# The skip weights of an S4D convolution, added by VectorE in SBUF in place of an identity matmul in PSUM

## The chip, the cores and the metric

The kernel runs on one core of one Trainium2 chip. Its five engines work side by side, each through its own queue of instructions in order: TensorE (PE in the profile; its weight loads are PEld), VectorE (DVE), ScalarE (ACT), GpSimd (POOL) and SyncE (SP, which here issues DMAs alone). The metric is the device time of one execution in microseconds (us).

## The reference

A layer norm of `x` (2048 tokens of 448 channels), and on its output `xn` two branches that are summed with `x`:

```python
xn = layernorm(x)
# branch A: a long convolution whose kernel comes from 256 complex modes per channel
A = -exp(log_A_real) + 1j * A_imag;  C = (C_real + 1j * C_imag) * dt
K = 2.0 * einsum("dn,dnl->dl", C, exp(A * dt * pos)).real      # 448 x 2048
y = irfft(rfft(xn, 2L) * rfft(K, 2L))[:L] + xn * D_skip
# branch B: a gated unit, 448 -> 1792 -> 448
h = (sigmoid(xn @ w_gate) * (xn @ w_up)) @ w_down
out = x + y + h
```

`xn * D_skip` is the same as adding `D_skip` to tap 0 of the convolution's kernel `K`, and that is how the kernel does it.

## The kernel before

Two generators in Python are traced in turns: `glu()` (branch B) and `conv()` (branch A). `conv` prepares the modes (`prep`), makes the kernels `K` (`kgen`), and then works in the frequency domain (`spectra`). Weights that are handed to the turns (`WK`, `WS` and others) decide how far one generator is traced before the other goes on. All instructions then get their place in their engine's queue from a planner that simulates the execution with its own costs: of the instructions that are ready it issues the one with the highest priority, which is the order of tracing, changed in places by `high_priority` blocks (`hp(HP)`) and by `issue_after` (behind a given instruction of the same engine). So the queue of an engine need not have the order of the code. Where an instruction needs what another engine has not finished, it waits at the head of its queue, and what is queued behind it waits too.

`kgen` makes the 448 kernels in 56 chunks of 8 channels, and 4 chunks make a bank of 32 channels, so there are 14 banks. Of a tap with index l = 64 a + b the two parts are made apart. For one chunk:

- GpSimd builds powers of the modes' magnitudes, `me` and `mf`, by doubling (`magnitudes`, L495 and L507), for two chunks at a time; ScalarE fills part of `me` by squares (L520).
- PE turns phases into angles (`ahead`, L529, tile `tr`), ScalarE takes sines (L537 to L540, tile `S`).
- DVE multiplies magnitudes by sines: `Et` in two instructions (L591, L592), `Ft` in one (L593). `Et` has two buffers, `Ft` has one.
- PE sums over the modes: 64 small matmuls into the PSUM tile `ko` (L607), 8 channels beside each other. `ko` holds a bank: 4 groups of 32 partitions (`a`) by 8 slots of 64 columns (`b`).

After the fourth chunk of a bank, the matmul at L617 adds the skip weights to the bank in PSUM: the stationary operand is a 128x128 identity, the moving one `dm[:, bank]`, 128x8, in which the rows 0, 32, 64 and 96 hold the `D_skip` of the bank's channels and all others are zero. It adds to column 0 of each slot, which with row 0 of each group is tap 0. ScalarE copies the bank to the SBUF tile `ks` (L620), of which there is one buffer. `first_stage` (L555) is the first step of the Fourier transform: 128 matmuls that read `ks`, traced two chunks later, or at once, with raised priority, for the last bank. ScalarE copies its results to `sk` (L561) and stores them in DRAM (L562). `spectra` loads them from there (`skl`) for the second step (L892).

Meanwhile `glu` has PE do the products of the gated unit, with its operands split into a high and a low part: L699 (tile `gu`) and L810 (tile `po`). On DVE it has the gate (L710), low parts of activations and weights (L717 `hl`, L754 `wl`) and the sums of the output (L815); on ScalarE the tanh (L707) and high parts (L715 `hh`, L750 `wh`); on GpSimd some weights' parts (L761, L762, L780).

Of the kernel before, what the change touches and what calls it, by code (L numbers as in the profile page):

```python
# [15 lines left out]
ALU = mybir.AluOpType  # L16
# [34 lines left out]
NCK = D // DC  # L51
# [77 lines left out]
def s4d_glu_kernel(ctx, tc, io):  # L129
    nc = tc.nc  # L130
    hp = tc.high_priority
    v = nc.vector
# [17 lines left out]
    ident = const.tile([128, 128], F32, name="ident")  # L150
# [10 lines left out]
    dm = const.tile([128, D // 32, 8], F32, name="dm")  # L161
# [272 lines left out]
    def powers(pms, g, fts, behind=None):  # L434

        w = W1s[0][:, NCH * g : NCH * g + NCH].rearrange("p g h e -> p (g h e)")
        pm = pms[g % 2]
        with tc.issue_after(behind.ins) if behind else nullcontext():
            nc.scalar.activation(pm[:, 0], w, AF.Identity, bias=one)
        for js, o in (((1, 2, 3), None), ((4, 5, 7), slice(1, 6)), ((8, 9), None), ((10, 11), slice(7, 12))):  # L440
            with tc.issue_after(fts[0].ins) if behind else nullcontext():
                for j in js:
                    v.scalar_tensor_tensor(pm[:, j], w, 2.0, w, ALU.add, ALU.mult)
                    w = pm[:, j]
                if o:
                    nc.scalar.activation(pm[:, o], pm[:, o], AF.Identity, bias=one)
            yield

    def kgen(pk):
# [11 lines left out]
        tl = {n: pk.tile(sh, dt_, name=n) for n, sh, dt_ in late}  # L461
# [22 lines left out]
        def magnitudes(b):  # L484

            c = 2 * b % NCH
            o = slice(2 * DC * c, 2 * DC * c + 4 * DC)
            pm = pms[2 * b // NCH % 2]
            par = lambda i: pm[:, i, o]
            me = mes[b % 2]  # L490
            mf = tl[f"mf{b % 2}"]
            gg = GGs[0][:, 2 * b : 2 * b + 2].rearrange("p c h e -> p (c h e)")

            with tc.issue_after(mls[0].ins) if mls else nullcontext():
                nc.gpsimd.tensor_tensor(  # L495
                    mf[:, :, 0:2],
                    gg.unsqueeze(2).to_broadcast([128, 4 * DC, 2]),
                    pm[:, 6:8, o].rearrange("p i m -> p m i"),
                    ALU.mult,
                )  # L500
            for m, base, nst in ((me, 0, 6), (mf, 7, 5)):
                for i in range(1 if m is mf else 0, nst):
                    w = 1 << i

                    a, n = (1, 2) if m is me and i > 3 else (0, 1)
                    with tc.issue_after(mls[0].ins) if mls else nullcontext():
                        ins = nc.gpsimd.tensor_tensor(  # L507
                            m[:, :, w + a : 2 * w : n],
                            m[:, :, a:w:n],
                            par(base + i).unsqueeze(2).to_broadcast([128, 4 * DC, w // n]),  # L510
                            ALU.mult,
                        )
            mls[:] = [ins]
            return me, mf

        def squares(me):

            with tc.issue_after(sins[0].ins) if sins else nullcontext():
                for w in (16, 32):
                    nc.scalar.activation(me[:, :, w : 2 * w : 2], me[:, :, w // 2 : w], AF.Square)  # L520

        def ahead(cn):


            S = tl[f"S{cn % 2}"]
            ps = psc[-1].tile([128, 2, 512], F32, name="tr", bufs=1)
            ph = pht[cn // 2 % 2]
            for h in range(2):
                nc.tensor.matmul(  # L529
                    ps[:, h], ph[:, cn % 2, 128 * h : 128 * h + 128], sel, start=True, stop=True  # L530
                )
            if cn % 2 == 1 and cn + 3 < NCK:
                phase_load(cn // 2 + 2)
            rows = lambda t: t.rearrange("p c (h e) s -> p h c (e s)", h=2)
            pv = ps.rearrange("p h (c x) -> p h c x", c=2)
            cs = S[:, 1:4:2]
            nc.scalar.activation(rows(cs), pv, AF.Abs)  # L537
            nc.scalar.activation(rows(S[:, 0:5:4]), pv, AF.Sin, scale=TWO_PI)
            nc.scalar.activation(rows(S[:, 2:3]), pv[:, :, 0:1], AF.Sin, scale=-TWO_PI)
            sins[:] = [nc.scalar.activation(cs, cs, AF.Sin, scale=-TWO_PI, bias=hpi)]  # L540
            return S

        def first_stage(bank):

            ks, sk = tl["ks"], tl["sk"].rearrange("p k (s r j) -> p r k s j", r=2, j=2)

            pss = [
                psc[-1].tile([128, 8, 2, 32], F32, name="kp", bufs=1),
                psg.tile([128, 8, 2, 32], F32, name="kq", tag="gu", bufs=4),
            ]  # L550
            for s_ in range(8):
                for cc in range(2):
                    for r in range(2):
                        rows = slice(64 * r, 64 * r + 64)
                        nc.tensor.matmul(  # L555
                            pss[r][64 * cc : 64 * cc + 64, s_].rearrange("p j k -> p (j k)"),
                            ks[rows, s_], wk[rows, cc], start=True, stop=True,
                            skip_group_check=True,
                        )
            for r in range(2):  # L560
                nc.scalar.copy(sk[:, r], pss[r].rearrange("p s j k -> p k s j"))  # L561
            nc.scalar.dma_start(sk_d[:, bank], tl["sk"])  # L562
# [11 lines left out]
        for g in range(NCK // NCH):  # L574
            for c in range(NCH):
                cn = g * NCH + c
                S = nxt
                me, mf = (m[:, 2 * DC * (c % 2) : 2 * DC * (c % 2) + 2 * DC] for m in mags)
                if c == 2 and NCH * (g + 1) < NCK:
                    more = powers(pms, g + 1, fts, sins[0])  # L580
                if 2 <= c < 6 and NCH * (g + 1) < NCK:
                    next(more)
                if cn + 1 < NCK:
                    nxt = ahead(cn + 1)
                    if c % 2 == 1:
                        squares(coming[0])
                yield WK / 3
                Et = tl[f"Et{cn % 2}"]
                Ft = tl["Ft"]
                two = lambda ap: ap.unsqueeze(1).to_broadcast([128, 2, 2 * DC, 32])  # L590
                v.tensor_tensor(Et[:, :, :, 32:64], two(me[:, :, 32:64]), S[:, 1::-1], ALU.mult)  # L591
                v.tensor_tensor(Et[:, :, :, 0:32], two(me[:, :, 0:32]), S[:, 1:3, :, ::-1], ALU.mult)  # L592
                fts[:] = [v.tensor_tensor(Ft, two(mf), S[:, 3:5], ALU.mult)]  # L593
                if cn + 2 < NCK and c % 2 == 0:
                    coming = magnitudes(cn // 2 + 1)
                if c % 2 == 1:
                    mags = coming
                yield WK / 3
                if cn % 4 == 0:
                    ko = psc[-1].tile([128, 8, 64], F32, name="ko", bufs=1)  # L600
                with tc.issue_after(glu_mm[0].ins):
                    for q in range(2):
                        sl = 2 * (cn % 4) + q
                        for k in range(4):
                            h, cc = k // 2, k % 2
                            for j in range(4):
                                nc.tensor.matmul(  # L607
                                    ko[32 * j : 32 * j + 32, sl],
                                    Ft[:, cc, DC * h + 4 * q + j],
                                    Et[:, cc, DC * h + 4 * q + j],  # L610
                                    start=(k == 0),
                                    stop=(k == 3),
                                    skip_group_check=True,
                                )
                if cn % 4 == 3:
                    ks = tl["ks"]
                    nc.tensor.matmul(  # L617
                        ko[:, :, 0], ident, dm[:, cn // 4], start=False, stop=True, skip_group_check=True
                    )
                    nc.scalar.copy(ks, ko)  # L620
                yield WK / 3
                if cn % 4 == 2 and cn > 3 or cn + 1 == NCK:

                    with hp(HP) if cn + 1 == NCK else tc.issue_after(glu_mm[0].ins):
                        first_stage((cn - 3) // 4 if cn + 1 < NCK else cn // 4)
# [520 lines left out]
```

## Time and profile before

| | |
|---|---|
| median of 3 runs | 735.8 us (734.0 to 740.97) |
| the profiled execution | 732.29 us |
| its span, first to last instruction | 730.4 us |
| PE busy | 679.1 us, 93% |
| DVE busy | 560.4 us, 77% |
| ACT busy | 421.1 us, 58% |
| POOL busy | 379.7 us, 52% |

The span is from the first to the last instruction of the profiled execution; 1.9 us lie around it. A row of the timeline has an instruction's start and length in us, its engine and line, what it writes and reads, and in brackets the idle time of its engine before it and what ended that. Lengths of matmuls overlap, since they are pipelined. A row of waits has who waited for whom, the total in us, how often, and the longest.

### The profile page before, as it was taken

What the parts mean: (1) busy time and instruction counts of PE and PEld (TensorE: products, weight loads), DVE (VectorE), ACT (ScalarE), POOL (GpSimd) and SP (SyncE); (2) the same over time, 40 slices, a digit from 0 to 9 for tenths busy, and PEclk for the clock granted to TensorE, in tenths of its full rate; (3) what the DMA queues carried; (4) which work ended last, traced back from release to release, by engine and by line L of the source; (5) the groups of instructions that cost most, each with busy time, mean ns of one, the idle gap of its engine ahead of it and who ended that gap; (6) DMA issues with size and microseconds to landing.
All of it is one profiled execution on the core that took longest, in us unless ns stands there. A gap on an engine that the chain in (4) does not pass through costs nothing.

```text
span 730.4 us, 19084 instructions
## 1 busy us (share of the span) xinstructions
PE 679.1 (93%) x7780; PEld 534.4 (73%) x7780; DVE 560.4 (77%) x776; ACT 421.1 (58%) x650; POOL 379.7 (52%) x423
## 2 busy tenths in 40 slices
PE   2998799997999999888999999999999999999994
PEld 1765688785887787555878887888877787776783
DVE  5799996798899999889579969977855555564553
ACT  3646364677688787888567778776742222323310
POOL 2120036798788987974655875876844002351001
PEclk9998999997999999999999999999999999999998
DMA  9946338326313562635863242232269999999746
GB/s 209 227 107 201 79 104 273 128 95 197 125 51 110 184 201 68 189 114 178 224 172 123 76 144 84 83 110 68 78 164 271 248 245 243 251 242 249 182 135 162
DMA packets 93288, 116.76 MB, mean 160 GB/s; under 512 B 12177, under 2 KB 81169, under 8 KB 92945
## 3 DMA queue, kind: packets, MB, share of 16 engines
q1 hardware_dynamic: 83888, 95.08, 47.9%
q10 hardware_dynamic: 6736, 14.57, 6.5%
q0 software_dynamic: 2576, 5.90, 3.5%
q8 instruction: 61, 1.00, 0.6%
q14 instruction: 27, 0.21, 0.1%
HBM read 70.75 MB, written 44.76 MB: 158 GB/s over the span
## 4 chain that ended last, share of the span: by engine, by line
PE 60%; DVE 10%; POOL 8%; DMA 8%; ACT 7%; issue 4%; SPq 2%; ACTq 1%; POOLq 0%; DVEq 0%
PE gu L699 23%; PE po L810 15%; PE sp L892 7%; PE ko L607 5%; PE pv L919 4%; PE tr L529 3%; POOL me L507 3%; POOL mf L507 2%; DMA wraw<-in_B_w_up_dram 1%; DVE wl L754 1%; POOL dl L780 1%; PE kp L555 1%; DMA acc<-in_A_u_dram 1%; DMA v_d<-vt 1%; DVE Et L591 1%
## 5 line engine op out<-in xcount | busy, mean ns | idle before, releaser
L507 POOL TENSOR_TENSOR me<-me,pm 128x32 f32<-128x32 f32 (+1 forms) x168 | 141.4, 841 | 89.6 <-DVE Et L592 77.6
L507 POOL TENSOR_TENSOR mf<-mf,pm 128x64 f32<-128x64 f32 (+1 forms) x112 | 127.1, 1135 | 4.7
L699 PE MATMUL gu<-xh,wh 128*128 128x512 f32 x336 | 101.8, 410 | 1.4 <-ACT xh L218 1.4
L699 PE MATMUL gu<-xh,wl 128*128 128x512 f32 x336 | 96.0, 393 | 0.0
L699 PE MATMUL gu<-xl,wh 128*128 128x512 f32 x336 | 95.8, 390 | 0.0
L591 DVE TENSOR_TENSOR Et<-me,S 128x1024 f32<-128x1024 f32 x56 | 82.6, 1475 | 10.1 <-ACT S L540 7.2
L810 PE MATMUL po<-dh,hh 128*128 128x448 f32 x224 | 86.0, 384 | 3.4 <-DVE acc L815 2.5
L810 PE MATMUL po<-dl,hh 128*128 128x448 f32 x224 | 84.3, 376 | 1.1 <-POOL dl L780 1.1
L592 DVE TENSOR_TENSOR Et<-me,S 128x1024 f32<-128x1024 f32 x56 | 77.0, 1375 | 10.1 <-ACT me L520 9.9
L593 DVE TENSOR_TENSOR Ft<-mf,S 128x1024 f32<-128x1024 f32 x56 | 78.3, 1398 | 7.0 <-POOL mf L507 3.1
L810 PE MATMUL po<-dh,hl 128*128 128x448 f32 x224 | 83.0, 373 | 0.0
L537 ACT ACTIVATE S<-tr 128x1024 f32<-128x1024 f32 x56 | 57.8, 1032 | 41.5 <-PE tr L529 39.5
L715 ACT CAST hh<-hf 128x512 fp32r<-128x512 f32 x56 | 34.9, 623 | 76.8 <-DVE hf L710 60.8
L699 PEld LDWEIGHTS gu<-xh,wh 128*128 128x128 f32 x336 | 62.4, 193 | 19.8 <-issue 3.4
L699 PEld LDWEIGHTS gu<-xh,wl 128*128 128x128 f32 x336 | 63.5, 189 | 15.1 <-DVE pl L306 0.7
L607 PEld LDWEIGHTS ko<-Et,Ft 128*32 128x32 f32 x3584 | 54.4, 111 | 26.7 <-issue 13.0
L699 PEld LDWEIGHTS gu<-xl,wh 128*128 128x128 f32 x336 | 63.0, 188 | 14.0 <-issue 0.7
L607 PE MATMUL ko<-Et,Ft 128*32 128x64 f32 x3584 | 64.5, 222 | 8.1 <-DVE Ft L593 6.3
L540 ACT ACTIVATE S<-S,hpi 128x1024 f32<-128x1024 f32 x56 | 65.5, 1170 | 2.9 <-DMA acc<-in_A_u_dram 2.9
L815 DVE SCALAR_TENSOR_TENSOR acc<-po,acc 128x448 f32<-128x448 f32 x80 | 48.5, 617 | 22.6 <-PE po L810 22.5
L717 DVE TENSOR_TENSOR hl<-hf,hh 128x512 fp32r<-128x512 f32 x56 | 49.6, 886 | 19.6 <-ACT hh L715 19.6
L710 DVE SCALAR_TENSOR_TENSOR hf<-th,gu 128x512 f32<-128x512 f32 x56 | 38.1, 681 | 31.1 <-PE gu L699 25.9
(196 smaller groups left out, 1284.2 us busy)
## 6 DMA issues: line engine op xcount, KB each, us to landing
sk_d<-sk ACTq DMA_DIRECT2D x14, 512.0 KB
sx<-x_d SPq DMA_DIRECT2D x32, 224.0 KB
skl<-sk_d SPq DMA_DIRECT2D x16, 448.0 KB
vp<-v_d SPq DMA_DIRECT2D x16, 448.0 KB
v_d<-vt SPq DMA_DIRECT2D x62, 112.0 KB
wt_d<-wh SPq DMA_DIRECT2D x9, 512.0 KB
wt_d<-wl SPq DMA_DIRECT2D x9, 512.0 KB
wl<-wt_d SPq DMA_DIRECT2D x9, 512.0 KB
```

The costliest lines, as they stand in the source:

```text
L507: ins = nc.gpsimd.tensor_tensor(m[:, :, w + a : 2 * w : n], m[:, :, a:w:n], par(base + i).unsqueeze(2).to_broadcast([128, 4 * DC, w // n]) ...
L537: nc.scalar.activation(rows(cs), pv, AF.Abs)
L540: sins[:] = [nc.scalar.activation(cs, cs, AF.Sin, scale=-TWO_PI, bias=hpi)]
L591: v.tensor_tensor(Et[:, :, :, 32:64], two(me[:, :, 32:64]), S[:, 1::-1], ALU.mult)
L592: v.tensor_tensor(Et[:, :, :, 0:32], two(me[:, :, 0:32]), S[:, 1:3, :, ::-1], ALU.mult)
L593: fts[:] = [v.tensor_tensor(Ft, two(mf), S[:, 3:5], ALU.mult)]
L607: nc.tensor.matmul(ko[32 * j : 32 * j + 32, sl], Ft[:, cc, DC * h + 4 * q + j], Et[:, cc, DC * h + 4 * q + j], start=(k == 0), stop=(k == ...
L699: glu_mm[:] = [nc.tensor.matmul(ps, a_, b_, start=(n == 0), stop=(n == len(mm) - 1))]
L717: v.tensor_tensor(hl, hf, hh, ALU.subtract)
L810: glu_mm[:] = [nc.tensor.matmul(po, a_[:, bs], w_, start=(n == 0), stop=(n == 3 * fc - 1))]
L815: v.scalar_tensor_tensor(acc[:, b], po, 0.5, acc[:, b], ALU.mult, ALU.add)
L892: mm = nc.tensor.matmul(to, tb[:kk, t, 64 * c : 64 * c + 64], rhs, start=True, stop=True, skip_group_check=True,)
```

## The change

The identity matmul goes. In its place DVE adds `dm[:, bank]` to column 0 of each slot of `ks`, in SBUF, after ScalarE's copy and before `first_stage` reads it. For all banks but the last, the add is traced in the next bank's first chunk, ahead of its `Et`; for the last bank it is traced after the copy, ahead of `first_stage`. It has no `issue_after` and no raised priority.

```diff
+        def skip(bank):
+            v.tensor_tensor(tl["ks"][:, :, 0], tl["ks"][:, :, 0], dm[:, bank], ALU.add)
+
...
                 yield WK / 3
+                if cn % 4 == 0 and cn:
+                    skip(cn // 4 - 1)
                 Et = tl[f"Et{cn % 2}"]
...
                 if cn % 4 == 3:
                     ks = tl["ks"]
-                    nc.tensor.matmul(
-                        ko[:, :, 0], ident, dm[:, cn // 4], start=False, stop=True, skip_group_check=True
-                    )
                     nc.scalar.copy(ks, ko)
                 yield WK / 3
+                if cn + 1 == NCK:
+                    skip(cn // 4)
                 if cn % 4 == 2 and cn > 3 or cn + 1 == NCK:
```

## The prediction

> **What bounds the kernel now.** I read the page from the top: busy shares, slices, then the chain that ended last.
>
> ```profile
> span 730.4 us, 19084 instructions
> PE 679.1 (93%) x7780; PEld 534.4 (73%) x7780; DVE 560.4 (77%) x776; ACT 421.1 (58%) x650; POOL 379.7 (52%) x423
> ...
> PE   2998799997999999888999999999999999999994
> ...
> DVE  5799996798899999889579969977855555564553
> ...
> PE 60%; DVE 10%; POOL 8%; DMA 8%; ACT 7%; issue 4%; SPq 2%; ACTq 1%; POOLq 0%; DVEq 0%
> ```
>
> TensorE (PE) is busy 93% of the span and carries 60% of the chain; VectorE (DVE) is nearly full in the first half and half empty in the last quarter. So I cut the span by stages. The kernel generation that the change touches runs from about 143 to 545 us; the columns are busy time of PE, its weight loads, DVE, ACT and POOL, then the granted clock, DMA share and GB/s.
>
> ```profile
> 143.00:300.00 157.00, 147.56 (x2237) 119.13 (x2236) 147.67 (x149) 121.30 (x177) 131.60 (x127) 0.97 0.41 131
> 300.00:345.00 45.00, 40.30 (x601) 26.28 (x595) 38.32 (x47) 38.20 (x64) 33.67 (x40) 0.96 0.50 147
> 345.00:545.00 200.00, 196.44 (x2991) 161.99 (x2991) 161.18 (x168) 140.42 (x202) 136.94 (x154) 0.99 0.40 120
> 545.00:650.00 105.00, 105.00 (x746) 80.34 (x745) 56.22 (x111) 30.50 (x58) 24.77 (x31) 1.00 1.03 250
> ```
>
> From 345 us PE is 98% busy and DVE 81%: PE time removed there is span removed. From 143 to 300 us both stand at 94%: there a microsecond taken from PE can be lost to DVE. Why DVE matters there is in the view of waits:
>
> ```profile
> POOL me L507 <- DVE Et L592: 77.6, 22, 8.9
> ```
>
> GpSimd, which makes the magnitudes for the next chunks, waits 77.6 us in all for DVE's products to free its buffer. Anything that delays an `Et` product on DVE goes round this loop.
>
> **What the change removes.** In each of 14 banks one matmul with the identity goes, which runs as two instructions.
>
> ```profile
> L617 PEld LDWEIGHTS ko<-dm,ident x28: 186/188/189, 167.1 to 541.5; 128*128 128x128 f32 x28
> L617 PE MATMUL ko<-dm,ident x28: 256/266/277, 167.1 to 541.6; 128*128 128x8 f32 x28
> ```
>
> The durations overlap, so I price it by starts, at one bank with it and one chunk without (PE's timeline, start and length):
>
> ```profile
> 194.07 1.10 PE L607 MATMUL ko<-Et,Ft 128*32 128x64 f32 x64
> 195.10 0.73 PE L529 MATMUL tr<-sel,ph 128*128 128x512 f32 x2
> ...
> 200.41 1.10 PE L607 MATMUL ko<-Et,Ft 128*32 128x64 f32 x64
> 201.44 0.39 PE L617 MATMUL ko<-dm,ident 128*128 128x8 f32 x2
> 201.69 0.48 PE L529 MATMUL tr<-sel,ph 128*128 128x512 f32 x1
> ```
>
> Without it the next work starts 195.10 - 194.07 = 1.03 us after the chunk's sums began, with it 201.69 - 200.41 = 1.28: 0.25 us for a bank, 14 x 0.25 = 3.5 us of PE time. How much lies on the path? The first and the last such piece in the chain, the first with what follows it:
>
> ```profile
> 201.51 0.32 PE ko L617 x2
> 201.83 0.57 PE tr L529 x2
> ...
> 513.92 0.32 PE ko L617 x2
> ```
>
> Banks 1, 4 and 6 to 12, counted from 0, have such a piece: nine, from the one at 201.51 to the one at 513.92. I take 9 x 0.25 = **-2.2 us**; bounds 0 and -3.5. The evacuation to `ks` (L620) can also start 0.3 us sooner, which I cost at nothing: the first stage that reads `ks` runs later anyway, apart from banks 0 and 13.
>
> **What the change adds: 14 small adds on DVE.** The trace has no such add on `ks`, but `x_scales` has ops of the same 128x8 size. In DVE's timeline, two that depend on each other, then a small one between strangers:
>
> ```profile
> 40.90 0.17 DVE L256 TENSOR_TENSOR z<-ys 128x8 f32<-128x8 f32 x1
> 41.10 0.17 DVE L257 SCALAR_TENSOR_TENSOR z<-z,ve 128x8 f32<-128x8 f32 x1
> ...
> 43.74 0.16 DVE L260 SCALAR_TENSOR_TENSOR zs<-mv,ys 128x8 f32<-128x8 f32 x1
> 43.82 1.22 DVE L754 TENSOR_TENSOR wl<-wraw,wh 128x1024 fp32r<-128x1024 f32 x1
> ```
>
> A small op holds DVE for 0.08 us when its neighbour doesn't need it and for 0.20 us when it does. The add's neighbours on DVE don't read `ks`, but it waits for ACT itself, so I take its length, 0.17. From 345 us on DVE has slack to hide it (81% busy); before 300 us it has not. Five banks (0 to 4) lie there: 5 x 0.17 = **+0.9 us**; bounds 5 x 0.08 = 0.4 and 14 x 0.20 = 2.8.
>
> The Trainium skill, "VectorE: DVE Perf Modes", section "The DRAIN you can't avoid", speaks against the change: the next op does not start until the pipe has emptied, so the count of ops is what to keep down. By that rule each add would cost its whole dependent step, 2.8 us in all; the 0.08 us step above doesn't bear it out between strangers, and the sum keeps its 0.9.
>
> **The wait that comes with it.** DVE takes its queue in order, so an add whose `ks` isn't there holds the products behind it. What matters is where the planner puts it: the code traces it ahead of the `Et` products of the next bank's first chunk, the planner issues what is ready. In bank 1 (ACT, then DVE, then PE):
>
> ```profile
> 201.87 0.59 ACT L620 COPY ks<-ko 128x512 f32<-128x512 f32 x1 [1.46 <-PE ko L617]
> ...
> 200.05 1.22 DVE L592 TENSOR_TENSOR Et<-me,S 128x1024 f32<-128x1024 f32 x1
> 201.18 1.44 DVE L591 TENSOR_TENSOR Et<-me,S 128x1024 f32<-128x1024 f32 x1
> 202.54 1.66 DVE L593 TENSOR_TENSOR Ft<-mf,S 128x1024 f32<-128x1024 f32 x1
> ...
> 204.96 0.27 PE L555 MATMUL kp<-wk,ks 64*64 64x64 f32 x1
> ```
>
> Both products of chunk 8 were issued before `ks` was done at 202.46. Issued by readiness, the add falls between L591 and L593 at 202.5: no wait on DVE, and 2.3 us before the first stage of this bank reads `ks`. So I cost the wait at nothing in the first 13 banks. If that cover went, the bank would lose what stands under the second rival.
>
> The last bank is different. ACT, DVE, GpSimd, PE, and for comparison the same DVE op one tile later:
>
> ```profile
> 541.28 0.62 ACT L715 CAST hh<-hf 128x512 fp32r<-128x512 f32 x1 [2.67 <-DVE hf L710]
> 541.85 0.59 ACT L620 COPY ks<-ko 128x512 f32<-128x512 f32 x1
> ...
> 541.93 2.65 DVE L717 TENSOR_TENSOR hl<-hf,hh 128x512 fp32r<-128x512 f32 x1 [0.69 <-ACT hh L715]
> 550.34 0.69 DVE L717 TENSOR_TENSOR hl<-hf,hh 128x512 fp32r<-128x512 f32 x1 [0.69 <-ACT hh L715]
> ...
> 541.66 2.36 POOL L762 TENSOR_TENSOR wl<-wraw,wh 128x1024 fp32r<-128x1024 f32 x1
> ...
> 542.49 0.27 PE L555 MATMUL kp<-wk,ks 64*64 64x64 f32 x1 [0.68 <-ACT ks L620]
> ```
>
> Here PE already stands idle for `ks`, and its first stage starts as soon as the copy ends (542.44). `hl` was ready at 541.90, ahead of `ks`, and has DVE until 544.58. The add comes behind it, ends near 544.7, and PE goes on at 544.7 in place of 542.5. From 545 to 650 us PE has no gap (105.00 us busy of 105.00 above), so nothing there gives the delay back: **+2.2 us**. The other end is +0.2, if the add goes before `hl`, or `hl` takes the 0.69 us that it took at 550. Why 2.65: GpSimd's subtraction ran beside it until 544.02.
>
> The Trainium skill, "GPSIMD Engine Reference", section "1. Specifications", says that GpSimd shares its SBUF interfaces with VectorE and that they contend where a DVE op has two SBUF inputs. Both ops here have two, and the rows agree (2.65 beside 0.69). By that rule the stretch returns after the change, since both ops stay; were it only chance, the sum would end 2.0 us lower.
>
> **Sum.** -2.2 + 0.9 + 2.2 = +0.9 us. The profiled execution took 732.29 us (730.4 of span and 1.9 around it), so 733.2 by its own measure. It ran 3.5 us under the median of the runs, 735.8; on that scale the forecast is **736.7**. Bounds of these terms: -3.5 + 0.4 + 0.2 = -2.9 and 0 + 2.8 + 2.4 = +5.2, that is 732.9 to 741.0.
>
> **The rivals.**
> 1. *PE's gain alone.* All fourteen identities pay (-3.5) and the last add slips in before `hl`, with DVE hiding the rest (+0.1): 732.4. For it: 94% PE already before 300 us. Against it: the chain has nine of the fourteen, and `hl` is ready first.
> 2. *The held queue (slower).* The add stands where the code has it, ahead of chunk 8's products. Chunk 7's `Ft` left DVE at 197.3:
>
> ```profile
> 195.95 1.33 DVE L593 TENSOR_TENSOR Ft<-mf,S 128x1024 f32<-128x1024 f32 x1
> ```
>
> DVE would then hold L592 from 200.05 to 202.6, 2.6 us; in 13 banks 34 us, less 2.2: 767. It decides from 0.6 us a bank on (13 x 0.6 is over 1%). Against it: DVE shows lines out of the order of the code all along (L592 ahead of L591 above).
> 3. *PE waits for the add (slower).* Bank 0 shows the pattern:
>
> ```profile
> 172.31 1.43 DVE L593 TENSOR_TENSOR Ft<-mf,S 128x1024 f32<-128x1024 f32 x1
> ...
> 172.50 0.37 PE L555 MATMUL kp<-wk,ks 64*64 64x64 f32 x1 [3.75 <-ACT ks L620]
> ```
>
> PE's first stage stood right at the copy's end; an add behind that `Ft` would let it start at 173.9, 1.4 us later. If the new plan puts all 13 so close, 18 us: 752. It needs a first stage within some 1.5 us of the copy; bank 1 has 2.5.
> 4. *The plan shifts.* The order of every engine is worked out anew from changed costs, and small shifts move other work, either way. What is at stake is PE's idle time: 45 - 40.30 = 4.7 us in 300 to 345, 157 - 147.56 = 9.4 before. A good shift: all identities pay and the 4.7 closes, 735.8 - 3.5 - 4.7 = 727.6. A bad one adds as much idle as the first stretch has: 735.8 + 0.9 + 9.4 = 746.1. Against the good side: PE is so full that there is little to win.
> 5. *It doesn't do what it says.* The identity is PE's only other work in this bank's sums and the diff deletes it; only its share of the path can fail, which is the bound of 0 above.
>
> **How the numbers follow.** Chances: forecast 0.45, rival 1 0.13, held queue 0.07, PE's wait 0.07, a bad shift 0.18, a good one 0.10. One per cent, about what these runs can tell from no change (734.0 to 740.97 without any), is 7.4 us: 728.4 to 743.2. So faster is the good shift, 0.10; within it the forecast and rival 1, 0.58; slower the rest, 0.32. The range goes from the good shift to a little past the bad one, 727.5 to 748, and leaves out rivals 2 and 3 (0.14). The forecast's own range is 732.9 to 741.0.
>
> **What the next profile would show.** No L617 on PE, and 1.03 us from a fourth chunk's sums to the next PE work: the first term. Fourteen new DVE ops of about 0.17 us on `ks`: the second. Their idle time before: next to none in banks 0 to 12 if readiness places them, some 2.6 us each if the held queue is right; PE's idle time before L555 growing by about 1 us a bank would be rival 3. Around the last copy, PE waiting for DVE some 2.9 us in place of 0.68: the third term. The forecast is wrong if PE's idle time in 143 to 545 us, 17.7 us now (9.4 + 4.7 + 3.6), changes by more than 5 us.

## The result, and the profile after

The changed kernel takes 761.25 us (median of four runs, 756.63 to 761.54), the kernel before 736.37 us beside it: a ratio of **1.031, 95% interval 1.026 to 1.035**, some 23 us slower (a run over 1.5% above the fastest of its kernel is left out of every ratio). The forecast was 736.7 us, in a range of 727.5 to 748. The changed kernel's profiled execution has a span of 754.9 us, 24.5 more than before's.

The head of its page: span, busy time by engine, the chain's shares.

```profile
span 754.9 us, 19049 instructions
PE 685.0 (91%) x7752; PEld 536.4 (71%) x7752; DVE 567.1 (75%) x790; ACT 421.1 (56%) x650; POOL 371.5 (49%) x423
...
PE 66%; DVE 11%; ACT 7%; DMA 6%; issue 5%; SPq 2%; POOL 1%; ACTq 1%; POOLq 0%; DVEq 0%
```

The edits are all there: PE has 28 instructions fewer (14 identities of two), DVE 14 more. The time went to two places. PE stands idle for 754.9 - 685.0 = 69.9 us, where before it was 730.4 - 679.1 = 51.3: **18.6 us more idle**. And PE is busy 5.9 us longer with less to do. The table by stages, same windows and columns as for before (lengths of busy time, then the granted clock, DMA share, GB/s), with one wide window added:

```profile
143.00:300.00 157.00, 138.14 (x2057) 112.92 (x2056) 141.29 (x146) 113.99 (x163) 122.10 (x126) 0.93 0.38 122
300.00:345.00 45.00, 41.06 (x594) 25.77 (x592) 40.68 (x47) 38.65 (x65) 33.19 (x39) 0.92 0.47 141
345.00:545.00 200.00, 192.76 (x2778) 155.89 (x2776) 157.16 (x171) 139.61 (x203) 129.71 (x147) 0.97 0.36 114
545.00:650.00 105.00, 100.88 (x941) 77.98 (x940) 60.23 (x104) 30.56 (x55) 25.32 (x32) 1.00 0.89 222
143.00:400.00 257.00, 229.59 (x3259) 176.53 (x3258) 212.83 (x227) 183.29 (x275) 180.14 (x196) 0.92 0.44 136
```

and before's wide window:

```profile
143.00:400.00 257.00, 240.29 (x3584) 187.39 (x3584) 225.72 (x237) 195.81 (x294) 196.96 (x205) 0.97 0.47 142
```

In 143 to 545 us PE now idles 18.86 + 3.94 + 7.24 = 30.0 us, where it was 17.7. The forecast named a change of more than 5 us there as what would make it wrong. Up to 400 us the idle time grew by 240.29 - 229.59 = 10.7 us, and the clock fell from 0.97 to 0.92. The trace records the granted clock as 1.0 or 0.5, so the means of the first three rows say how long it stood at 0.5: (157 x 0.07 + 45 x 0.08 + 200 x 0.03) / 0.5 = 41 us, where the rows of before give 17. The end of ScalarE's copy to `ks` shows how the delay builds up (after less before, in us, worked out from the two traces, banks 0 to 13):

```
+4.2  +6.2  +5.7  +6.6  +6.9  +7.2  +14.1  +17.7  +18.5  +17.9  +17.8  +17.6  +18.0  +20.4     end of span +24.5
```

Three steps: some 5 us by bank 1, some 10 between banks 5 and 7, some 6 from bank 12 to the end.

**The first step.** PE has its longest idle time there. ScalarE, then PE, of the changed kernel (start, length, what it does, and in brackets the idle time before it and what ended that):

```profile
164.49 0.60 ACT L539 ACTIVATE S<-tr 128x512 f32<-128x512 f32 x1
171.75 1.04 ACT L754 CAST wh<-wraw 128x1024 fp32r<-128x1024 f32 x1 [6.66 <-DMA wraw<-in_B_w_up_dram]
...
176.06 0.55 ACT L622 COPY ks<-ko 128x512 f32<-128x512 f32 x1
...
178.82 1.16 ACT L540 ACTIVATE S<-S,hpi 128x1024 f32<-128x1024 f32 x1
...
180.00 1.94 PE L612 MATMUL ko<-Et,Ft 128*32 128x64 f32 x64 [10.15 <-ACT S L540]
...
183.02 0.37 PE L558 MATMUL kp<-wk,ks 64*64 64x64 f32 x1
```

and ScalarE in the kernel before:

```profile
163.48 0.60 ACT L539 ACTIVATE S<-tr 128x512 f32<-128x512 f32 x1
167.57 1.05 ACT L750 CAST wh<-wraw 128x1024 fp32r<-128x1024 f32 x1 [3.49 <-PE ko L617]
```

In both kernels ScalarE stands at the same weight cast, ahead of sines that PE needs, and PE runs dry meanwhile. Two things differ.

- *The stall ends later.* The cast starts at 171.75, 4.2 us later than before (167.57). After the change the profile says that it waited for the load of the weights; in before's row it names PE's identity, which the cast doesn't need, so there the load is only the likelier cause. This delay can't come from the order of the queues: up to bank 0's first stage they are the same on every engine, apart from the identity. It differs from profile to profile: against before, bank 0's copy ends 0.8 us later in `new_order_identity`, 1.6 in `add_raised` and 6.2 in `old_order_none` (all below), and that last one has the old order.
- *The stall is filled with less.* Before, PE had bank 0's first stage as soon as the copy ended (its row at 172.50 stands in the prediction), with 3.75 us idle ahead of it. After, the sums of chunk 4 stand ahead of the first stage in PE's queue, and they need the sines: PE does nothing until 180.00, though `ks` had been copied at 176.61. Here the first stage couldn't have gone first either: its add stands behind an `Et` in DVE's queue and ends at 179.93. Without any add, in `new_order_identity`, the copy ends at 173.26 and PE starts with the sums at 176.49: the order alone costs 3.2 us there.

So the queues have **another order**. Compared instruction by instruction (identity and add left out), so many stand at another place than before:

```
PE 2153 of 4924    DVE 167 of 776    ACT 256 of 716    POOL 88 of 419    SP 114 of 541
```

The first difference in time, on any engine, is the swap that the rows above show.

**The second step** is the largest. One place in it shows the same pattern. ScalarE, DVE and PE of the changed kernel:

```profile
383.72 0.62 ACT L719 CAST hh<-hf 128x512 fp32r<-128x512 f32 x1 [8.66 <-issue]
...
384.37 0.69 DVE L721 TENSOR_TENSOR hl<-hf,hh 128x512 fp32r<-128x512 f32 x1 [6.27 <-ACT hh L719]
...
386.25 1.93 PE L612 MATMUL ko<-Et,Ft 128*32 128x64 f32 x64 [3.96 <-DVE Ft L598]
```

and of the kernel before:

```profile
367.19 0.62 ACT L715 CAST hh<-hf 128x512 fp32r<-128x512 f32 x1 [5.86 <-issue]
...
367.84 0.69 DVE L717 TENSOR_TENSOR hl<-hf,hh 128x512 fp32r<-128x512 f32 x1 [5.55 <-ACT hh L715]
...
369.72 1.10 PE L607 MATMUL ko<-Et,Ft 128*32 128x64 f32 x64 [0.77 <-DVE Ft L593]
```

In both, ScalarE stalls and DVE waits with `Ft` queued behind; before, PE had products of the gated unit to fill all but 0.77 us of it, after it runs dry for 3.96. The same gap is 3.30 us in `new_order_identity` and 3.52 in `old_then_new`, so it goes with the new order and needs no add. The rest of this step, between banks 5 and 6, isn't traced to rows here, apart from 10 us at a clock of 0.50 (last section).

**The adds.** The group's row (count, then busy time and mean ns of one, then DVE's idle time before them), and three rows of waits:

```profile
L544 DVE TENSOR_TENSOR ks<-ks,dm 128x8 f32<-128x8 f32 x14 | 9.5, 678 | 0.0
```

```profile
POOL me L507 <- DVE Et L597: 88.2, 19, 14.2
...
PE ko L612 <- ACT S L540: 10.2, 1, 10.2
```

```profile
  PE kp L558: 6.3, 3
```

GpSimd's wait for `Et` grew from 77.6 us to 88.2; it is 87.9 in `new_order_identity`, without adds, so the adds didn't make it. The last row is from the view of the add's own line: PE waited for it three times, 6.3 us in all. DVE never idled ahead of an add (0.0), so nothing was held behind one that had to wait. But each add takes 678 ns on average, four times the 0.17 us of the forecast. Bank 2 shows both, DVE, then GpSimd, then PE:

```profile
237.21 2.07 DVE L597 TENSOR_TENSOR Et<-me,S 128x1024 f32<-128x1024 f32 x1
239.21 1.09 DVE L544 TENSOR_TENSOR ks<-ks,dm 128x8 f32<-128x8 f32 x1
...
238.17 2.10 POOL L784 TENSOR_TENSOR dl<-rd,dh 128x448 fp32r<-128x448 f32 x1
...
240.35 0.27 PE L558 MATMUL kp<-wk,ks 64*64 64x64 f32 x1 [2.69 <-DVE ks L544]
```

The add began while GpSimd was inside an instruction that ended at 240.27, and ended itself at 240.30.

### The profile page after: what moved, and what is told of

The parts are those of the page before. It is cut to its first block, busy times and chain, and to the rows that moved or that the text cites. A ratio compares the mean times of both kernels' runs of the same rounds, so it can differ in the third digit from the quotient of the medians.

```text
span 754.9 us, 19049 instructions
## 1 busy us (share of the span) xinstructions
PE 685.0 (91%) x7752; PEld 536.4 (71%) x7752; DVE 567.1 (75%) x790; ACT 421.1 (56%) x650; POOL 371.5 (49%) x423
## 4 chain that ended last, share of the span: by engine, by line
PE 66%; DVE 11%; ACT 7%; DMA 6%; issue 5%; SPq 2%; POOL 1%; ACTq 1%; POOLq 0%; DVEq 0%
PE gu L703 28%; PE po L814 14%; PE sp L896 7%; PE ko L612 6%; PE pv L923 4%; PE tr L529 3%; DVE Ft L598 2%; DVE hl L721 1%; PE kp L558 1%; PE kq L558 1%; ACT S L538 1%; ACT S L537 1%; PE gu L278 1%; ACT S L540 1%; DVE Et L597 1%
## 5 line engine op out<-in xcount | busy, mean ns | idle before, releaser
L507 POOL TENSOR_TENSOR me<-me,pm 128x32 f32<-128x32 f32 (+1 forms) x168 | 144.1, 858 | 108.1 <-DVE Et L597 88.2
L507 POOL TENSOR_TENSOR mf<-mf,pm 128x64 f32<-128x64 f32 (+1 forms) x112 | 116.0, 1036 | 5.8
L597 DVE TENSOR_TENSOR Et<-me,S 128x1024 f32<-128x1024 f32 x56 | 77.8, 1390 | 15.3 <-ACT me L520 13.1
L596 DVE TENSOR_TENSOR Et<-me,S 128x1024 f32<-128x1024 f32 x56 | 78.7, 1407 | 8.0 <-ACT S L540 7.9
L612 PE MATMUL ko<-Et,Ft 128*32 128x64 f32 x3584 | 66.4, 228 | 17.8 <-ACT S L540 10.2
L612 PEld LDWEIGHTS ko<-Et,Ft 128*32 128x32 f32 x3584 | 56.2, 114 | 35.6 <-issue 12.1
```

What stands on the lines that cost most here:

```text
L507: ins = nc.gpsimd.tensor_tensor(m[:, :, w + a : 2 * w : n], m[:, :, a:w:n], par(base + i).unsqueeze(2).to_broadcast([128, 4 * DC, w // n]) ...
L612: nc.tensor.matmul(ko[32 * j : 32 * j + 32, sl], Ft[:, cc, DC * h + 4 * q + j], Et[:, cc, DC * h + 4 * q + j], start=(k == 0), stop=(k == ...
```

## The experiments

Most of them hold the order of the queues fixed. To pin one, every instruction got an edge of issue order to the one that is to stand ahead of it on its engine; this moves no data and adds no wait between engines (in outline):

```diff
+    for engine, queue in want.items():          # the order recorded from another build
+        for a, b in zip(queue, queue[1:]):
+            tc.add_manual_dep(b, a.name, no_sync, reason="pinned")
```

"Old order" is that of the kernel before, "new order" that of the changed one. Each ratio is to the kernel before on the same chip.

### The order or the add?

The changed program in the old order, each add behind the DVE instruction that ran when the copy ended:

> The changed kernel (no identity, 14 adds on DVE) with every queue held in the order that the kernel before had; each add stands behind the DVE instruction that was in flight when its copy ended, the last one behind the low part of the activations. Theory O (the time went into the new order of the queues): 733 to 740 us, the forecast's own range, since identity, adds and the last wait are then all that is left (-3.5 to +5). Theory A (the adds themselves cost it: 9.5 us on DVE in the profile after, and the first stage waits for them): 748 us or more.

The program before, with its identities, in the new order:

> The kernel before (identity on PE, no add on DVE) with every queue held in the order that the changed kernel has; each identity stands right behind its bank's last sum. Theory O: the loss is there without any add, 752 to 766 us. Theory A: 734 to 742 us. If it is halfway, about 748, both have a part.

The first took 738.02 us, ratio 1.002 (0.999 to 1.005). The second took 754.4 us, ratio **1.021** (1.015 to 1.027), without one add. Its page and its wide window:

```profile
span 753.3 us, 19092 instructions
...
PE 691.9 (92%) x7780; PEld 541.5 (72%) x7780; DVE 564.0 (75%) x776; ACT 421.8 (56%) x650; POOL 379.6 (50%) x423
```

```profile
143.00:400.00 257.00, 236.46 (x3286) 181.10 (x3285) 212.41 (x222) 186.29 (x279) 187.53 (x195) 0.91 0.44 137
```

PE has all its identities again and is late in the same places: 20.5 us idle in the wide window (before: 16.7) at a clock of 0.91, and 6.91 us idle in one piece in front of chunk 4's sums. Over the whole span PE idles 753.3 - 691.9 = 61.4 us, 10.1 more than before, and is busy 12.8 us longer with the very same instructions, for which the lower clock is the likely cause. So about two thirds of the loss (2.1 of 3.1%) is the order alone; the share is rough, since either interval is about a point wide. The remaining 1.0%, 7 us, comes with the adds in that order. PE waits 6.3 us for them, which is about as much, but no run isolates that.

### What the parts cost in the old order

Identity and add both left out, so without the skip weights, in the old order:

```diff
-            v.tensor_tensor(tl["ks"][:, :, 0], tl["ks"][:, :, 0], dm[:, bank], ALU.add)
+            pass
```

> Neither identity nor add (the skip weights are left out of the computation), queues in the order of the kernel before. It measures the first term, the identity on PE: the forecast said -2.2 us with bounds 0 and -3.5, so 732 to 736 us. The difference of old_order_adds to it is the price of the 14 adds with the order held: theory O says +3 (0.9 and 2.2), theory A at least +12.

733.86 us, ratio 0.998 (0.994 to 1.002): the identities are worth 0.24% or 1.8 us, with an interval that reaches from a gain of 4.7 to a loss of 1.2.

As `old_order_adds`, with the last bank's add ahead of `hl` in DVE's queue:

> As old_order_adds, but the last bank's add stands ahead of the low part of the activations on DVE. By the forecast's third term the last first stage then waits 0.2 us and not 2.2 for it: 2.0 us less than old_order_adds. If the wait is hidden after all, no difference; if the low part itself is needed at once, slower.

737.85 us, ratio 1.001 (0.998 to 1.004): no difference to `old_order_adds` that can be told. Why it doesn't pay is in the rows, ScalarE, DVE, GpSimd, PE:

```profile
546.12 0.58 ACT L624 COPY ks<-ko 128x512 f32<-128x512 f32 x1
546.73 1.60 DVE L545 TENSOR_TENSOR ks<-ks,dm 128x8 f32<-128x8 f32 x1 [1.17 <-ACT ks L624]
...
545.97 2.33 POOL L768 TENSOR_TENSOR wl<-wraw,wh 128x1024 fp32r<-128x1024 f32 x1
...
548.39 0.36 PE L560 MATMUL kp<-wk,ks 64*64 64x64 f32 x1 [2.58 <-DVE ks L545]
```

The add is first now, and it is the add that is stretched: it ends 0.03 us after GpSimd's subtraction (548.30), and PE waits 2.58 us in place of the 3.18 that it waits in `old_order_adds`.

An add that reads the bank from PSUM and writes column 0 of `ks`, while ScalarE copies the other 63 columns, without the identity and again in the old order:

```diff
-                    nc.scalar.copy(ks, ko)
+                    v.tensor_tensor(ks[:, :, 0], ko[:, :, 0], dm[:, cn // 4], ALU.add)
+                    nc.scalar.copy(ks[:, :, 1:], ko[:, :, 1:])
```

> DVE adds the skip weights while it reads column 0 of the bank from PSUM and writes it to ks; ScalarE copies the other 63 columns; no identity; queues in the order of the kernel before. In the two traces with adds on ks, each add that began while GpSimd was in an instruction ended 0.03 us after that instruction, 0.2 to 2.35 us long; the DVE ops with one input in PSUM (L815) all took 607 to 626 ns. Theory S (a DVE op with two SBUF inputs waits out GpSimd's instruction): all 14 adds near 0.17 us, no wait of the last first stage beyond 0.9 us, and 733 to 736 us, the time of old_order_none. If the stretch has another cause: adds of up to 1 us again and about 738.

738.55 us, ratio 1.001 (0.997 to 1.006). The stretch is gone (durations are least, median, most of the 14, in ns), also where GpSimd is busy throughout, as at 437 us:

```profile
L618 DVE TENSOR_TENSOR ks<-ko,dm x14: 157/172/177, 170.6 to 546.9; 128x8 f32<-128x8 f32 x14
```

```profile
437.05 1.07 POOL L508 TENSOR_TENSOR me<-me,pm 128x512 f32<-128x512 f32 x1
437.59 0.17 DVE L618 TENSOR_TENSOR ks<-ko,dm 128x8 f32<-128x8 f32 x1 [2.12 <-PE ko L608]
```

The adds' 6.8 us of DVE in `old_order_adds` became 2.4, and PE's wait at the last bank 0.93 us. So theory S was right on the cause of the stretch. Its 733 to 736 us were not met: the time didn't move measurably against `old_order_adds`. That doesn't show that the stretch was covered there, since this add has waits of its own: DVE idles 7.6 us ahead of it, in 8 places, until PE's sums are done, and ScalarE's copies wait 5.6 us for it.

### Any new order, or this one?

The same program as `old_order_none`, with the planner free:

> Neither identity nor add (skip weights left out of the computation), and the planner free to order the queues. Theory L (the order before was an especially good one, and any new order costs 1 to 3%): 742 to 757 us. Theory D (what spoils the new order is that the first stage depends on a late add on DVE): 730 to 737, as with the old order.

743.07 us, ratio 1.009 (1.006 to 1.013), against 0.998 pinned: the same instructions lose 1.2% by being ordered anew. So less work on PE made the kernel slower, through the order.

The PSUM add, with the planner free:

> As psum_add_old_order with the planner free; the add is traced beside the copy. Theory D: the add no longer follows the copy, so 734 to 740. Theory L: 742 to 757 whatever the add does.

741.8 us, ratio 1.007 (1.003 to 1.010), just under theory L's range and just above theory D's.

The kernel before with its identities and 14 adds on a scratch tile besides, planner free:

```diff
+    dj = const.tile([128, 8], F32, name="dj")
...
+                    v.tensor_tensor(dj, dm[:, cn // 4], dm[:, 0], ALU.add)
```

> The kernel before with its identity, and beside it 14 adds of the same size on DVE into a tile that nobody reads, traced at the copy; the planner free. Nothing waits for these adds. Theory L: 742 to 757. Theory D: 737 to 742, the adds' own time alone.

744.81 us, ratio 1.011 (1.008 to 1.014). This one says little: needing nothing from the bank, all 14 adds were issued between 9.9 and 13.5 us, before the kernel generation, and the kernel is some 7 us late already when PE has done its first 20 us of work. As a sample of a changed plan it goes with the others; the price of an add it doesn't give.

The change with one edit, the add traced right behind its copy, with raised priority:

```diff
                     nc.scalar.copy(ks, ko)
+                    with hp(HP):
+                        skip(cn // 4)
```

> The change with one edit: the add is traced right behind the copy of its bank, with raised priority, in all 14 banks; the queues are the planner's. If the order is the main cost and any re-planning draws a new one (the three re-planned kernels so far: 1.007 to 1.011), it comes out between 1.005 and 1.02, and the PE waits for the add shrink below 6.3 us. If the late adds are the main cost, it comes back to the old order's 1.002. If it beats the kernel before (under 0.995), the adds' place was all.

Four runs took 752.4 to 766.76 us, too far apart for an interval; the lowest is 2.0% over the 737.53 of before. Its adds take 9.5 us in all and PE waits 6.7 us for them, as without the edit; PE stands idle for 7.22 us at the same place of bank 0. Raising the add doesn't help: it stays in the new kind of order, at or above the upper end of what that theory expected, and PE's waits for the add did not shrink, as that theory had it.

### Where in the order

The changed program once more, with the two orders joined at the copy of bank 4 (about 290 us):

> The changed program with every queue pinned: up to the copy of bank 4 in the order of the changed kernel, behind that in the order of the kernel before (adds there behind the DVE instruction that ran when the copy ended). In the two traces the changed kernel is 6.9 us behind at that copy, and 24.5 us at the end. Theory A, the order of each stretch costs what is lost in that stretch: about 7 us over before, 744, ratio 1.009. Theory B, one early swap (chunk 4's sums ahead of bank 0's first stage, 10 us of idle PE behind it) puts everything out of step and the rest follows from it: 755 or more, 1.025. Theory C, only the later stretch matters: within 3 us of before, 1.003 at most.

> The complement: up to the copy of bank 4 the order of the kernel before with the adds, behind that the order of the changed kernel. Theory A: what the changed kernel loses behind that copy, 24.5 - 6.9 = 17.6 us, less or more the 1 us that the adds cost in the old order: 754, ratio 1.023. Theory B: about 739, ratio 1.003, since the early swap is gone. Theory C: as A, 754 or more.

New, then old: 747.52 us, ratio 1.011 (1.005 to 1.016). Old, then new: 757.73 us by the median of the three runs that count, ratio 1.028 (1.020 to 1.036). Each stretch of the new order costs by itself. That one early swap sets off all the rest falls: with the old order up to bank 4 the loss behind it is still there, and larger. The two losses together, less the 0.2% of the old order counted twice, make 1.1 + 2.8 - 0.2 = 3.7%, near the 3.1% of the whole, within their intervals. That only the later stretch matters falls too, but it has the larger share. There the copies to `ks` end 0.2 us later than before at bank 4, 12.2 at bank 7, 12.1 at bank 12 and 17.3 at the last bank.

## Why the prediction was wrong

**The sum came out for the order in which it was reckoned.** There the change costs +0.2% or 1.5 us (-0.7 to +3.8), forecast +0.9. The interval is 4.5 us wide, and one term was mis-sized, so this doesn't prove the terms one by one.

- Identities, -2.2: measured -1.8, well within the bounds of 0 and -3.5, though the interval is wider than they are.
- Adds, +0.9: sized wrongly, 6.8 and 9.5 us of DVE time in all, where 14 x 0.17 is 2.4. The prediction had quoted the stretch of `hl` beside GpSimd and did not apply it to the add, which also has two SBUF operands. In the old order no difference in time can be told (2.4 against 6.8 us of DVE, 1.001 against 1.002). The rule of the Trainium skill, "VectorE: DVE Perf Modes", section "The DRAIN you can't avoid", against which this term was weighed, is not tested by that: 2.8 us or 0.9, none of the runs could tell. The same section adds that a next op that is not held starts earlier, so the 0.08 us step isn't against it.
- Last bank, +2.2: came out. ScalarE, DVE, PE of the changed kernel:

```profile
562.25 0.58 ACT L622 COPY ks<-ko 128x512 f32<-128x512 f32 x1
562.37 2.61 DVE L721 TENSOR_TENSOR hl<-hf,hh 128x512 fp32r<-128x512 f32 x1 [0.68 <-ACT hh L719]
564.90 0.16 DVE L544 TENSOR_TENSOR ks<-ks,dm 128x8 f32<-128x8 f32 x1
565.12 0.27 PE L558 MATMUL kp<-wk,ks 64*64 64x64 f32 x1 [3.18 <-DVE ks L544]
```

  PE waits 3.18 us in place of 0.68: +2.5, for the reason given; whether all of it reached the span, the runs can't tell. The stretch of `hl` returned (2.61), as the prediction took from the Trainium skill, "GPSIMD Engine Reference", section "1. Specifications"; but the other end that it gave, +0.2 with the add ahead of `hl`, does not exist as long as GpSimd's subtraction runs, as `old_order_last_first` showed.

**The step that failed** is that the sum worked on in before's order, as if only the add were put in, and gave the new order of the queues nothing. That order by itself, with the identities and without an add, costs 2.1%, some 15 us (11 to 20). A smaller miss is the step "So I cost the wait at nothing in the first 13 banks": PE waits 3.1 us there, in banks 1 and 2. Bank 1 was the example; what the changed kernel did there, ScalarE, DVE, PE:

```profile
208.02 0.60 ACT L622 COPY ks<-ko 128x512 f32<-128x512 f32 x1
...
210.27 1.21 DVE L597 TENSOR_TENSOR Et<-me,S 128x1024 f32<-128x1024 f32 x1
211.40 0.16 DVE L544 TENSOR_TENSOR ks<-ks,dm 128x8 f32<-128x8 f32 x1
...
211.62 0.27 PE L558 MATMUL kp<-wk,ks 64*64 64x64 f32 x1 [0.41 <-DVE ks L544]
```

The add came right behind the second `Et`, 2.8 us after the copy's end and not at once; the cover of 2.3 us was gone and PE waited 0.41. Alone that is small, and DVE held nothing: the held queue (rival 2) did not occur. PE's wait for the add (rival 3) occurred in three places, not 13, 6.3 us and not 18. What happened is **rival 4, the bad shift of the plan**: seen, given 0.18, and priced too low. Its price was one stretch's idle time, 9.4 us, taken once, on the ground that a shift adds about as much idle as lies there. The runs show a loss in each of the two stretches that were joined, and a price in PE's clock that the rival did not have at all: of what the new order alone adds to the profiled span, 12.8 us are PE's longer busy time and 10.1 idle time. Against a good shift the argument held: none of the re-planned kernels won.

What turned the plan over, the identity's PE time gone or the add between copy and first stage, is not settled in full. `none_free` says that the first alone is enough for 1.2%. The add counts too: chunk 4's sums stand ahead of bank 0's first stage in the two free plans with an add on `ks` (the change and `add_raised`, 2% and more over before), and behind it in `none_free` and `psum_add_free` (0.9 and 0.7%).

## What to carry to other kernels

Where a planner orders the queues, a small edit is two changes: its own work, which can be summed from rows, and a new draw of the order, which here cost some ten times that sum (15 us against 1.5). Pinning the old order onto the new program separates the two, and tells whether an idea or its schedule lost. When PE is 93% busy, price a bad draw by the stalls that some queue already has (a cast that waits for a load, say) and by what work now fills them: that is what a swap can uncover.

## What the runs showed of the hardware

**A small VectorE operation can wait out a GpSimd instruction.** An add of 128x8 with both inputs in SBUF takes 0.16 us while GpSimd is idle; if it begins while GpSimd is computing, it ends when that instruction does. In the profiles of the changed kernel and of `old_order_adds`, 20 of the 28 adds began inside such an instruction; 19 ended 0.03 us behind it, and one, with 0.04 us of it left, took its 0.16. An add inside GpSimd's issue of a DMA took 0.16 us too. The longest of the changed kernel, GpSimd and DVE:

```profile
537.47 3.36 POOL L766 TENSOR_TENSOR wl<-wraw,wh 128x1024 fp32r<-128x1024 f32 x1
538.51 2.35 DVE L544 TENSOR_TENSOR ks<-ks,dm 128x8 f32<-128x8 f32 x1
```

They end at 540.83 and 540.86. With one input in PSUM the same add took 157 to 177 ns throughout, in eight cases with over 0.2 us of a GpSimd instruction left. So the price of the add with two SBUF inputs isn't its size, but what is left of GpSimd's instruction.

**The clock falls around PE's idle times, though not around all, and not there alone.** Slices of the changed kernel, columns as above:

```profile
170.00:180.00 10.00, 0.00 (x1) 0.03 (x1) 7.17 (x8) 8.22 (x12) 4.37 (x7) 0.71 0.57 191
180.00:190.00 10.00, 10.00 (x184) 8.03 (x188) 7.63 (x8) 7.20 (x11) 6.76 (x9) 0.78 0.45 157
240.00:250.00 10.00, 6.76 (x135) 5.31 (x136) 6.76 (x7) 9.08 (x14) 9.30 (x12) 0.66 0.35 112
344.90:355.10 10.20, 10.20 (x86) 7.11 (x83) 5.82 (x8) 5.26 (x10) 5.39 (x5) 0.50 0.32 71
```

After the 10.15 us gap the sums of a chunk took 1.94 us (row at 180.00), where at full clock they take 1.10: the idle time is paid again in part by what follows. The Trainium skill, "TensorE: Matmul & The Clock Gate", section "HAM oscillation — how this bites in real kernels", warns of idle gaps of more than some 3.4 us. The long gap agrees; but the slice from 240 us has 0.66 with gaps of 2.69 and 2.89 us around it, and the window from 545 to 650 us has 1.00 in spite of a gap of 3.18. In `old_order_adds` a gap of 3.18 us at the same place is followed by a clock of 0.50 (548.7 to 552.0 us). And it is 0.50 from 344.9 to 355.1 us, though PE has no gap over 0.4 us in the 15 us ahead. No run isolates what sets the clock here.
